# Issuing the FFN weight loads from ScalarE instead of SyncE, with a new order for all engines

## The chip, the cores and the metric

The kernel runs on one core of a Trainium2 chip. The metric is device time in microseconds (us) of one execution, lower being better. Shown of the kernel before are three timed runs, with a median of 195.04 us (192.67 to 195.28), and one profiled execution of its own, of 195.64 us, whose instructions span 193.9 us.

TensorE (PE) multiplies matrices, VectorE (DVE), ScalarE (ACT) and GpSimd (POOL) do element-wise work, and SyncE (SP) issues DMA transfers. ScalarE can issue them too. Each engine takes its own instructions strictly in the order in which they were written. Data that passes between engines is guarded by semaphores: an instruction carries the waits that must be met before it starts.

## What is computed

```
state = 0                                          # per batch (4) and head (8): 48 x 48
for t in range(768):
    cur   = (u * k[t]) outer v[t]
    y[t]  = r[t] @ (state + cur)
    state = w[t][:, None] * state + k[t] outer v[t]
x   = y as 3072 tokens x 384                       # 4 batches x 768 steps, 8 heads x 48
out = relu(x @ w_in) ** 2 @ w_out                  # w_in 384 x 2048, w_out 2048 x 384
```

So a recurrent attention layer is followed by a feed-forward network (FFN). Everything is given and returned in float32.

## The kernel before

**Tiling.** The 3072 tokens are cut into 24 steps of 128 tokens. For each step the attention part works on chunks: it loads w, r, k and v (192 KB each, L150), takes logarithms (`lw`) and cumulative sums by a matmul (`cum`), exponentials (`ci`, `exp`), scales r and k (`rd`), transposes them (`tr`, copied out by `rkt`), multiplies and masks (`p`, `pm0`, `pm1`), updates the state (`su`, `ac`, `ts`, `sn`) and forms y (`ys`, `ye`, plus the term with u by `ku`, `qp`, `q`, `vq`; summed in `ysb`). y is transposed (`yt`) and copied into `xT` (`xt`).

The FFN works on 17 blocks: ten of one step and seven of two. For a block, `m1:i:g` is a group of matmuls against `w_in` that fills one bank of PSUM (L405; 12 matmuls for a block of one step), `rl` takes it out with a relu (L414 on ACT, L416 on DVE), `gt` squares it, and `m2:i:mt:q` multiplies four of sixteen slices by `w_out` (L435). `os` scales the result out of PSUM and `store` writes it. There are two PSUM buffers for `m1`, so a third group can only start when the `rl` of the first has been done.

**FFN weights.** They come in eight loads of 768 KB. `ld:0:i` to `ld:3:i` (below wi0 to wi3; `load_wi`, L174 to L178) each bring a quarter of the columns of `w_in`; `ld:0:o` to `ld:3:o` (wo0 to wo3; `load_wo`, L180 to L184) each bring a quarter of the rows of `w_out`. They land in a staging pool of six float32 buffers, and `cast:i:g:j` (three per load) and `cast:o:g:j` (four per load) turn them into bf16 on ACT, DVE or POOL. Group g of `m1` in a block of one step needs the three casts of wi*g*, and quarter q of `m2` needs the four casts of wo*q*. As the pool has six buffers, wo2 and wo3 wait until wi0 and wi1 have been cast.

**Order.** A string, `ORDER`, lists every piece of work as a word; the function `tile_rwkv6_finch__then__act_relu_squared_kernel` reads it word by word under `tc.manual_schedule`. So each engine gets its instructions in the order of the words that concern it. A last letter picks the engine (A for ACT, V or W for DVE, G for POOL). `warm:n` puts n matmuls on zeros on PE as filler (`warm:n:1` has half a matmul more). All loads are issued from SP, in the order of the `ld` words; the `store` words stand in the same queue.

**Completion semaphores.** The framework gives every DMA one of eight completion semaphores in turn. An issue carries a wait on the previous DMA that had the same semaphore: that one must have landed. In the kernel before, all these DMAs are issued by SP (but for one half of the last store), so each waits for the eighth DMA ahead of it on its own queue. The raw tiles of w, r, k and v have seven buffers each.

Of the kernel before, what the change touches and what calls it, by code (L numbers as in the profile page):

```python
# [26 lines left out]
m1:2:2 gt:0:2:A cast:i:3:1:V ld:2:o rl:1:2:A cum:4 ye:3 ci:4 ac:3 m1:1:3 ld:3:o rl:2:2:A ku:4:G ysb:3 gt:1:2:A
ts:3 m1:2:3 ld:4:v rl:1:3:A gt:2:2:V qp:4:G yt:3 ld:5:w rl:2:3:A xt:3:V m1:0:3 exp:4 m1:3:0 sn:3:G q:4
rl:0:3:A rd:4 cast:o:0:1:G cast:o:0:2:A m1:3:3 cast:o:0:3:A cast:o:0:0:V gt:0:3:V tr:4 gt:1:3:A m2:0:0:0
gt:2:3:A rkt:4:V cast:o:1:1:G rl:3:0:A m2:1:0:0 ld:6:w cast:o:1:0:V rl:3:3:A cast:o:1:3:G ys:4 cast:o:1:2:V  # L30
p:4 gt:3:0:A m1:3:2 pm0:4 gt:3:3:A cast:o:2:1:G m1:3:1 cast:o:2:0:A pm1:4 rl:3:2:A cast:o:2:3:G m2:0:0:1
rl:3:1:V cast:o:2:2:G m2:1:0:1 ld:5:r gt:3:2:W gt:3:1:A ld:5:k m2:0:0:2 cast:o:3:2:G cast:o:3:0:A ld:7:w
cast:o:3:3:A m2:1:0:2 v:4:V vq:4:G ld:6:r cast:o:3:1:A ye:4 su:4 lw:5 m2:0:0:3 ysb:4 ac:4 ts:4 cum:5 m2:1:0:3
os:0:0:A ci:5 lw:6 ld:6:k yt:4 sn:4:V m2:2:0:0 exp:5 m2:2:0:1 xt:4:A ld:8:w os:1:0:A m2:2:0:2 rd:5 ku:5:G
ld:5:v m2:2:0:3 qp:5:G lw:7 cum:6 tr:5 os:2:0:V ld:6:v m2:3:0:0 ci:6 rkt:5:A q:5 m1:4:0 ld:9:w exp:6 ku:6:V
ys:5 m1:4:2 ld:7:r rl:4:0:A qp:6:G rd:6 m2:3:0:1 lw:8 store:0:0 gt:4:0:A m2:3:0:2 rl:4:2:V ld:7:k v:5:A vq:5:G
p:5 q:6 gt:4:2:A tr:6 ld:8:r pm0:5 m1:4:1 vq:6:G pm1:5 ld:8:k m2:4:0:0 rkt:6:V rl:4:1:A cum:7 v:6:V gt:4:1:A
ye:5 ld:7:v m2:3:0:3 ci:7 ysb:5 exp:7 m2:4:0:1 yt:5 os:3:0:A ld:9:r m1:4:3 xt:5:V rd:7 ku:7:G su:6 rl:4:3:A
m1:5:0 ld:9:k ac:6 qp:7:G p:6 gt:4:3:A sn:6 m1:5:2 ld:10:r rl:5:0:A pm0:6 ku:8:G lw:9 tr:7 pm1:6 ld:10:k
rl:5:2:A m2:4:0:2 gt:5:0:W rkt:7:A qp:8:G cum:8 ye:6 q:7 ld:11:r m2:4:0:3 ysb:6 gt:5:2:A vq:7:G m1:5:1 q:8  # L40
v:7:A ld:12:r ci:8 ys:7 yt:6 rl:5:1:A ku:9:G m2:5:0:0 xt:6:V store:1:0 exp:8 gt:5:1:W su:7 ld:11:k qp:9:G
m1:6:0 ac:7 rd:8 store:2:0 m2:5:0:1 rl:6:0:A ku:10:V m2:5:0:2 gt:6:0:A ld:8:v ts:7 qp:10:G p:7 q:9 m1:6:1
ld:9:v pm0:7 sn:7:G ld:12:k m1:5:3 pm1:7 rl:6:1:A tr:8 os:4:0:A q:10 ld:10:w gt:6:1:A m1:6:2 rl:5:3:A ku:11:G
cum:9 ye:7 ci:9 rl:6:2:A m2:6:0:0 ysb:7 store:3:0 gt:5:3:A qp:11:G m1:6:3 ld:13:r gt:6:2:W exp:9 m2:5:0:3
vq:8:G ld:11:w rl:6:3:V v:8:A m2:6:0:1 rd:9 rkt:8:A vq:9:G store:4:0 m2:6:0:2 q:11 v:9:G gt:6:3:A ys:8 yt:7
ld:13:k os:5:0:A p:8 ku:12:G xt:7:V m2:6:0:3 ld:10:v pm0:8 lw:10 su:8 pm1:8 qp:12:G m1:7:0 ld:14:r ac:8
os:6:0:V cum:10 ts:8 ye:8 rl:7:0:A m1:7:2 ld:14:k ci:10 sn:8:G gt:7:0:A tr:9 ysb:8 rl:7:2:A m1:7:1 q:12 exp:10
rkt:9:V ld:11:v m1:7:3 rl:7:1:A ku:13:G rd:10 yt:8 ys:9 rl:7:3:A ld:12:v m2:7:0:0 gt:7:2:A xt:8:V qp:13:G p:9
gt:7:3:A su:9 ld:12:w pm0:9 m1:8:0 vq:10:G ac:9 pm1:9 lw:11 m1:8:3 ld:13:w gt:7:1:A v:10:G ts:9 cum:11
rl:8:0:A q:13 ye:9 sn:9:G tr:10 ld:14:w rl:8:3:A ci:11 m1:8:1 ysb:9 gt:8:0:A ku:14:G store:5:0 m2:7:0:1  # L50
rkt:10:V exp:11 ld:15:r v:11:G m1:8:2 gt:8:3:A rd:11 ld:15:k qp:14:G yt:9 rl:8:1:A ys:10 m2:8:0:0 xt:9:V
v:12:A ld:13:v gt:8:1:W vq:11:G lw:12 su:10 p:10 ac:10 rl:8:2:V m2:7:0:2 vq:12:G lw:13 ld:16:r ts:10 gt:8:2:A
m2:7:0:3 pm0:10 sn:10:G lw:14 tr:11 pm1:10 os:7:0:A ld:17:r m2:8:0:1 rkt:11:A q:14 ye:10 cum:12 ld:16:k
m2:8:0:2 ysb:10 ku:15:G ci:12 yt:10 m2:8:0:3 ld:14:v xt:10:V exp:12 qp:15:G m1:9:0 os:8:0:A ld:18:r rd:12
m1:9:2 rl:9:0:A vq:13:G ys:11 q:15 ld:17:k m1:9:1 rl:9:2:A v:13:G gt:9:0:V gt:9:2:A su:12 p:11 ld:15:w
rl:9:1:A m1:9:6 pm0:11 ku:16:G ac:12 gt:9:1:A pm1:11 m1:9:3 ld:15:v rl:9:6:A sn:12 qp:16:G ye:11 m2:9:0:0
rl:9:3:A ysb:11 ld:18:k gt:9:6:A tr:12 gt:9:3:V vq:14:G q:16 m1:9:5 v:14:A store:6:0 rkt:12:A store:7:0
m2:9:1:0 ku:17:G rl:9:5:V ld:16:w m1:9:7 gt:9:5:A qp:17:G p:12 lw:15 ld:16:v yt:11 pm0:12 m1:9:4 rl:9:7:A
pm1:12 m2:9:1:1 ld:19:r rl:9:4:A xt:11:V ld:19:k cum:13 q:17 gt:9:4:A ye:12 m2:9:0:1 ci:13 v:15:A ysb:12
m2:9:0:2 exp:13 gt:9:7:W store:8:0 vq:15:G yt:12 ld:17:w m2:9:1:2 rd:13 xt:12:A ld:17:v m2:9:1:3 ku:18:V  # L60
cum:14 su:13 os:9:1:V qp:18:G ld:18:v m1:10:0 lw:16 ci:14 ac:13 m1:10:2 exp:14 ts:13 ld:20:r m2:9:0:3 q:18
# [447 lines left out]
```

## Time and profile before

| What | Value |
|---|---|
| Three timed runs | 192.67, 195.04, 195.28 us |
| Profiled execution, its own time | 195.64 us |
| Its span, first to last instruction | 193.9 us |
| PE busy | 186.4 us (96%) |
| DVE busy | 155.6 us (80%) |
| ACT busy | 141.5 us (73%) |
| POOL busy | 86.8 us (45%) |
| Moved by DMA | 30.24 MB |
| Mean granted TensorE clock | 1.000 |

The busy time of an engine is the time in which it executes; waiting and issuing DMAs are not in it. The span is divided into 40 slices in the page of the profile, and digits show in tenths how busy an engine was in each. A timeline shows an engine's instructions in order, runs of equal ones merged: start, length, line, tiles and count. SPq stands for the issue of a DMA by SP. In the chain of work that ended last, each step is followed back to what released it.

### The profile page before, as it was taken

What the parts mean: (1) busy time and instruction counts of PE and PEld (TensorE: products, weight loads), DVE (VectorE), ACT (ScalarE), POOL (GpSimd) and SP (SyncE); (2) the same over time, 40 slices, a digit from 0 to 9 for tenths busy, and PEclk for the clock granted to TensorE, in tenths of its full rate; (3) what the DMA queues carried; (4) which work ended last, traced back from release to release, by engine and by line L of the source; (5) the groups of instructions that cost most, each with busy time, mean ns of one, the idle gap of its engine ahead of it and who ended that gap; (6) DMA issues with size and microseconds to landing.
All of it is one profiled execution on the core that took longest, in us unless ns stands there. A gap on an engine that the chain in (4) does not pass through costs nothing.

```text
span 193.9 us, 5430 instructions
## 1 busy us (share of the span) xinstructions
PE 186.4 (96%) x2164; PEld 138.5 (71%) x2164; DVE 155.6 (80%) x285; ACT 141.5 (73%) x279; POOL 86.8 (45%) x115
## 2 busy tenths in 40 slices
...
DMA  6999998989998979899999899922000101001121
GB/s 135 211 236 317 260 248 247 367 192 198 212 220 172 243 154 224 169 206 224 228 242 205 173 206 205 229 51 81 3 0 21 63 0 59 29 3 41 41 73 52
DMA packets 107180, 30.24 MB, mean 156 GB/s; under 512 B 100370, under 2 KB 105619, under 8 KB 107155
## 3 DMA queue, kind: packets, MB, share of 16 engines
...
q10 hardware_dynamic: 144, 0.10, 0.2%
...
## 4 chain that ended last, share of the span: by engine, by line
PE 62%; SPq 16%; DMA 8%; POOL 5%; ACT 3%; issue 3%; DVE 1%; POOLq 0%
PE m L435 26%; PE m L405 22%; SPq L150 11%; DMA v_raw<-in_v_dram 5%; PE tr L302 4%; DMA rk_raw<-in_k_dram 3%; PE cp L314 3%; SPq L176 2%; SPq L182 2%; PE y L374 2%; PE tr L387 2%; POOL qprod L190 2%; POOL ku L190 2%; PE cp L272 1%; PE y L363 1%
## 5 line engine op out<-in xcount | busy, mean ns | idle before, releaser
L405 PE MATMUL m<-xT,wi_sb 128*128 128x128 bf16 (+1 forms) x816 | 75.3, 241 | 0.4 <-DVE xT L187 0.2
L435 PE MATMUL m<-wo_sb,gt 128*128 128x384 bf16 x384 | 73.1, 326 | 0.5 <-POOL wo_sb L187 0.5
L405 PEld LDWEIGHTS <-wi_sb 128*128 128x128 bf16 x816 | 59.2, 98 | 7.7 <-issue 0.5
L414 ACT ACTIVATE rl<-m 128x512 f16<-128x512 f32 x73 | 42.6, 594 | 10.6 <-PE m L405 9.8
L435 PEld LDWEIGHTS <-gt 128*128 128x128 bf16 x384 | 35.3, 98 | 18.3 <-issue 0.7
L426 ACT ACTIVATE gt<-rl 128x512 bf16<-128x512 f16 x61 | 37.5, 629 | 4.4 <-DVE rl L416 3.5
L326 DVE TENSOR_TENSOR pmT<-cp,tri_strict 128x512 bf16<-128x512 f32 x48 | 30.9, 683 | 3.9 <-PE cp L314 3.7
L190 POOL TENSOR_TENSOR ku<-rk_raw,u_bc 128x384 f32<-128x384 f32 x20 | 20.6, 1029 | 15.9 <-DMA rk_raw<-in_k_dram 14.9
L190 POOL TENSOR_TENSOR qprod<-rk_raw,ku 128x384 f32<-128x384 f32 x23 | 23.1, 1003 | 8.4 <-DVE ku L190 7.1
L283 ACT ACTIVATE cp<-cp 128x768 f32<-128x768 f32 x24 | 19.2, 799 | 10.2 <-DVE cp L276 10.1
L190 POOL TENSOR_TENSOR vq<-v_raw,q 128x384 f32<-128x384 f32 x22 | 18.4, 841 | 16.7 <-DVE y_sb L379 12.7
L293 DVE TENSOR_TENSOR rdec_buf<-rk_raw,cp 128x768 bf16<-128x768 f32 x24 | 22.8, 949 | 2.5 <-ACT cp L283 1.7
L190 POOL TENSOR_TENSOR S<-t_state,ac_buf 128x384 bf16<-128x384 f32 x13 | 11.1, 855 | 22.1 <-DVE t_state L349 22.0
L416 DVE TENSOR_SCALAR rl<-m 128x512 f16<-128x512 f32 x23 | 15.7, 686 | 6.0 <-PE m L405 4.9
L276 DVE SCALAR_TENSOR_TENSOR cp<-cp,lw_buf 128x384 f32<-128x384 f32 x24 | 13.4, 560 | 4.6 <-PE cp L272 4.6
L246 ACT ACTIVATE lw_buf<-w_raw 128x384 bf16<-128x384 f32 x24 | 12.4, 521 | 4.4 <-DMA w_raw<-in_w_dram 2.2
L453 PE MATMUL m<-warm 128*128 128x512 bf16 (+1 forms) x50 | 14.2, 424 | 1.3 <-DVE warm L220 1.3
L302 PE MATMUL tr<-ident,rdec_buf 128*128 128x128 bf16 x192 | 14.7, 219 | 0.1
L262 DVE TENSOR_REDUCE q<-qprod 128x8 f32<-128x384 f32 x24 | 13.1, 545 | 2.0 <-POOL vq L190 2.0
L379 DVE TENSOR_TENSOR y_sb<-vq,y 128x384 bf16<-128x384 f32 x24 | 13.2, 548 | 1.6 <-PE y L374 0.8
L302 PEld LDWEIGHTS <-rdec_buf 128*128 128x128 bf16 x192 | 11.9, 98 | 2.5 <-issue 0.7
L187 ACT COPY rkT<-tr 128x1024 bf16<-128x1024 bf16 x12 | 12.1, 1006 | 1.4 <-PE tr L302 1.4
...
## 6 DMA issues: line engine op xcount, KB each, us to landing
...
```

Source lines behind the costliest of these rows:

```text
L150: nc.sync.dma_start(out=dst, in_=src[b, :, c * C:(c + 1) * C, :].rearrange("h c d -> c h d"))
L190: {"V": nc.vector, "G": nc.gpsimd}[eng].tensor_mul(dst, a, b)
L283: nc.scalar.activation(cs[:, :, 0:DM], cs[:, :, 0:DM], AF.Exp)
L293: nc.vector.tensor_mul(rdec[:, :, :, 0:D], raw["rk", s][:], tiles.pop(("cs", s))[:, :, 0:DM].rearrange("p a (h d) -> p a h d", h=H))
L302: nc.tensor.transpose(ps_tr[:, i, p, :], rdec[:, i, 2 * p:2 * p + 2, :], ident[:])
L326: nc.vector.tensor_mul(tiles["pmT", s][:, e], tiles["p", s][:, e].rearrange("p (a t) -> p a t", a=HP), tri_strict[:, None, :].to_broadcast ...
L405: nc.tensor.matmul(ps1[:, j, :], wi_sb[:, kk, n * 128:(n + 1) * 128], xT[:, kk, s0 * C:s0 * C + width], start=(kk == 0), stop=(kk == KT - 1))
L414: nc.scalar.activation(rl[:], m1[:], AF.Relu, scale=RS)
L416: nc.vector.tensor_scalar(rl[:], m1[:], RS, 0.0, op0=ALU.mult, op1=ALU.max)
L426: nc.scalar.activation(gt, rl[:], AF.Square)
L435: nc.tensor.matmul(tiles["m2", i, mt][:], gt[:, n, mt * 128:(mt + 1) * 128], wo_sb[:, n, :], start=(n == 0), stop=(n == NT - 1))
L453: nc.tensor.matmul(ps[:, 0:256 if i == n else 512], warm[:, 0:C], warm[:, 0:256 if i == n else 512], start=True, stop=True)
```

## The change

Two things change. `load_wi` and `load_wo` issue their transfers by `nc.scalar.dma_start` where they had `nc.sync.dma_start`. So the eight weight loads stand in ACT's instruction order, and travel on ACT's DMA queue. And the string `ORDER` is a new one: the pieces of work are the same, but the order on every engine, the engine of many casts, relus and copies, and the fillers differ (50.5 filler matmuls in 13 places, where there were 48.5 in nine). No other line changes.

```diff
-ld:0:w ld:0:r warm:7 ld:0:k ld:1:r ld:0:u lw:0 cum:0 warm:9:1 ld:0:v ci:0 ld:1:w exp:0 ld:2:w rd:0 ub warm:2
-uc:A ld:2:r ld:1:k v:0:G tr:0 ld:2:k ku:0:G warm:3 rkt:0:V lw:1 qp:0:G su:0 lw:2 cum:1 ld:1:v warm:11 ac:0
-ci:1 sn:0 ld:2:v ku:1:G exp:1 q:0 ld:0:i rd:1 vq:0:G qp:1:V cum:2 tr:1 ku:2:G ld:3:w ci:2 warm:5 q:1 ld:1:i
-exp:2 rkt:1:V v:1:G ld:3:r rd:2 qp:2:G ld:3:k su:1 warm:1:1 ac:1 v:2:A ts:1 p:0 vq:1:G q:2 su:2 pm0:0 sn:1:G
-warm:4:1 ac:2 pm1:0 vq:2:G ld:2:i ts:2 ye:0 cast:i:0:0:A p:1 cast:i:0:1:G ysb:0 tr:2 cast:i:0:2:A sn:2:V ys:1
-lw:3 warm:5 pm0:1 rkt:2:A pm1:1 ld:3:v yt:0 ye:1 ld:3:i cast:i:1:1:G cast:i:1:2:A p:2 xt:0:V ysb:1 m1:0:0
...
+ld:0:w ld:0:u warm:5:1 ld:0:r ld:0:k ld:1:w ld:1:r ub lw:0 ld:0:v cum:0 uc:A warm:11 ci:0 ld:1:k exp:0 ku:0:G
+ld:1:v ld:0:i rd:0 lw:1 ld:2:w qp:0:V tr:0 q:0 cum:1 warm:5:1 rkt:0:A ld:2:r ci:1 exp:1 v:0:V ld:3:r vq:0:V
+su:0 warm:5 ac:0 rd:1 ku:1:G ld:3:w sn:0 p:0 qp:1:G v:1:A pm0:0 tr:1 warm:2 pm1:0 rkt:1:A q:1 ye:0 warm:0:1
+ysb:0 vq:1:G p:1 cast:i:0:2:A ld:2:k su:1 pm0:1 ys:1 cast:i:0:0:G ac:1 warm:2:1 pm1:1 lw:2 ld:3:k ld:1:i
+cast:i:0:1:G ts:1 ye:1 cum:2 ysb:1 yt:0 ld:2:v ld:2:i sn:1:G warm:3:1 ci:2 ld:3:i xt:0:V exp:2 ld:3:v yt:1
+m1:0:0 xt:1:V lw:3 m1:1:0 ld:4:w ld:0:o warm:5 rl:0:0:A rd:2 ku:2:G ld:4:r rl:1:0:A gt:0:0:A qp:2:G cum:3 tr:2
+gt:1:0:A ci:3 warm:3 rkt:2:V exp:3 ku:3:G q:2 ys:2 warm:4 rd:3 qp:3:G cast:i:1:0:A ld:4:k p:2 cast:i:1:2:G
+cast:i:1:1:A q:3 tr:3 pm0:2 ld:1:o v:2:G m1:1:1 ld:2:o rkt:3:V ld:3:o vq:2:G m1:0:1 pm1:2 rl:1:1:A su:2
+gt:1:1:V rl:0:1:A p:3 ye:2 cast:i:2:2:V cast:i:2:0:A warm:1:1 cast:i:2:1:V ac:2 ysb:2 m1:1:2 gt:0:1:A ts:2
...
     def load_wi(g):
         w_st["i", g] = stage_pool.tile([C, KT, GW], FP32, name="w_st")
-        nc.sync.dma_start(
+        nc.scalar.dma_start(
             out=w_st["i", g][:],
             in_=moe_w_in[:, g * GW:(g + 1) * GW].rearrange("(a p) f -> p a f", p=128))
 
     def load_wo(g):
         w_st["o", g] = stage_pool.tile([C, 4, DM], FP32, name="w_st")
-        nc.sync.dma_start(
+        nc.scalar.dma_start(
             out=w_st["o", g][:],
             in_=moe_w_out[g * 512:(g + 1) * 512, :].rearrange("(a p) d -> p a d", p=128))
```

With this, the eight completion semaphores are shared by two issuing engines. In the built program the weight loads, issued by ACT, take their turns between loads issued by SP, and each carries the wait for the DMA that had its semaphore before. The table names it, and what stands on ACT between one weight load and the next (w2 is the load of w for step 2, and so on):

| Weight load | Waits until this has landed | ACT's work up to the next one |
|---|---|---|
| wi0 | r0 | `lw:1`, `rkt:0`, `exp:1`, `ac:0`, `v:1`, `rkt:1`, `cast:i:0:2`, `ac:1`, `lw:2` |
| wi1 | r2 | none |
| wi2 | k2 | none |
| wi3 | v3 | `exp:2`, `lw:3` |
| wo0 | k4 | `rl:0:0`, `rl:1:0`, `gt:0:0`, `gt:1:0`, `exp:3`, `cast:i:1:0`, `cast:i:1:1` |
| wo1 | r5 | none |
| wo2 | r6, and POOL's cast of wi0 | none |
| wo3 | r7, and the casts of wi1 by ACT and POOL | `rl:1:1`, `rl:0:1`, `cast:i:2:0`, `ac:2`, and so on |

SP's loads now stand in this order: w0, u, r0, k0, w1, r1, v0, k1, v1, w2, r2, r3, w3, k2, k3, v2, v3, w4, r4, k4, v4, w5, w6, r5, k5, r6, k6, v5, r7, k7, v6, w7, w8, v7, r8, and then the first store. Those among them that wait for a weight load are w4 (for wi0), r5 (wi1), r6 (wi2), r7 (wi3), w7 (wo0), and the first store (wo1).

More of the change, by code (lines that the diff above doesn't have):

```diff
@@ L27 @@
[L27 to L61, printed above, removed]
@@ new lines @@
+m1:0:2 pm0:3 rl:1:2:A sn:2:G yt:2 pm1:3 cast:i:3:1:A ld:4:v cast:i:3:0:G ys:3 xt:2:A warm:1:1 rl:0:2:V
+cast:i:3:2:A m1:2:0 ld:5:w vq:3:G v:3:V gt:0:2:A m1:2:1 lw:4 gt:1:2:V ye:3 rl:2:0:A cum:4 su:3 ysb:3 rl:2:1:A
+m1:0:3 ci:4 gt:2:0:A m1:2:2 rl:0:3:V gt:2:1:A cast:o:0:1:G ld:6:w cast:o:0:0:A rl:2:2:V m1:2:3 cast:o:0:3:G
+ac:3 gt:0:3:A ts:3 m1:1:3 ld:5:r cast:o:0:2:G rl:2:3:A gt:2:2:V yt:3 sn:3:G rl:1:3:A m2:0:0:0 xt:3:V gt:2:3:W
+exp:4 m2:1:0:0 ku:4:G gt:1:3:A m1:3:0 rd:4 qp:4:G m1:3:2 rl:3:0:V cast:o:1:3:A tr:4 cast:o:1:2:A cast:o:1:0:V
@@ new lines @@
+cast:o:1:1:G m1:3:1 q:4 rl:3:2:A rkt:4:V gt:3:0:A m1:3:3 rl:3:1:A gt:3:2:V cast:o:2:2:G m2:0:0:1 cast:o:2:0:V
+cast:o:2:3:A cast:o:2:1:A ys:4 p:4 rl:3:3:A m2:1:0:1 pm0:4 gt:3:1:A pm1:4 m2:1:0:2 cast:o:3:0:G cast:o:3:1:A
+ld:5:k cast:o:3:3:V cast:o:3:2:A m2:0:0:2 gt:3:3:W v:4:A m2:0:0:3 ld:6:r vq:4:V ye:4 su:4 os:0:0:V lw:5 ld:6:k
+m2:1:0:3 ac:4 ysb:4 cum:5 ts:4 m2:2:0:0 os:1:0:A ld:5:v ci:5 sn:4:G yt:4 m2:2:0:1 exp:5 xt:4:V ld:7:r m1:4:0
+rd:5 ku:5:G m1:4:1 lw:6 ld:7:k rl:4:0:A m2:2:0:2 qp:5:V rl:4:1:A ld:6:v cum:6 gt:4:0:V tr:5 gt:4:1:A ci:6
@@ new lines @@
+qp:11:G rl:7:0:A m1:7:1 ac:8 q:10 m1:7:3 gt:7:0:A v:9:G ts:8 ld:12:w rl:7:1:A p:8 vq:9:G q:11 tr:9 os:5:0:A
+pm0:8 rl:7:3:A m1:7:2 sn:8:G ld:13:k pm1:8 v:10:A m2:7:0:0 vq:10:G lw:10 rkt:9:V store:3:0 rl:7:2:A ye:8
+ld:14:r cum:10 gt:7:3:V su:9 gt:7:1:A ci:10 m2:6:0:3 store:4:0 ac:9 gt:7:2:W lw:11 m2:7:0:1 ysb:8 exp:10
+ku:12:G ld:14:k m2:7:0:2 ts:9 rd:10 ys:9 yt:8 sn:9:G m2:7:0:3 v:11:A ld:15:r xt:8:A cum:11 ld:12:v qp:12:G
+tr:10 ci:11 os:7:0:A m1:8:0 rkt:10:V vq:11:G exp:11 ld:13:w m1:8:2 q:12 rl:8:0:A rd:11 su:10 rl:8:2:A m1:8:1
@@ new lines @@
+ku:13:G gt:8:0:A ld:13:v os:6:0:V p:9 lw:12 m1:8:3 pm0:9 qp:13:G rl:8:1:A ld:14:w pm1:9 m2:8:0:0 ac:10
+gt:8:2:A ts:10 ye:9 ld:15:w p:10 gt:8:1:A q:13 sn:10:G tr:11 rl:8:3:A ysb:9 m2:8:0:1 ld:15:k rkt:11:A pm0:10
+ku:14:G ys:10 m2:8:0:2 pm1:10 gt:8:3:A ld:14:v qp:14:G ye:10 cum:12 yt:9 ysb:10 m2:8:0:3 xt:9:A vq:12:G
+ld:16:r ci:12 ys:11 q:14 yt:10 exp:12 v:12:G xt:10:V ld:16:k lw:13 m1:9:0 rd:12 v:13:A vq:13:G m1:9:5
+store:5:0 rl:9:0:V ld:17:r p:11 rl:9:5:A tr:12 gt:9:0:V ld:15:v lw:14 pm0:11 m1:9:2 gt:9:5:A pm1:11 ld:17:k
@@ new lines @@
+rl:10:4:A ld:18:v ys:14 qp:20:V gt:10:7:A tr:15 v:16:G ld:22:r p:14 gt:10:4:A m2:10:1:1 pm0:14 rkt:15:A
+vq:16:G ld:22:k pm1:14 m2:10:1:2 q:19 m2:10:0:2 ld:19:v yt:13 ye:14 cum:16 xt:13:A m2:10:0:3 ysb:14 v:17:A
+ci:16 yt:14 ys:15 ld:20:v os:10:0:V m2:10:1:3 xt:14:A exp:16 vq:17:V m1:11:0 store:9:1 q:20 os:10:1:A ku:21:G
+store:10:0 su:15 rd:16 rl:11:0:A m1:11:1 ld:21:v ac:15 m1:11:3 gt:11:0:A qp:21:G ts:15 lw:18 rl:11:1:V p:15
+ld:23:r tr:16 rl:11:3:A sn:15:G pm0:15 gt:11:1:A m1:11:2 pm1:15 ld:21:w rkt:16:A m1:11:6 rl:11:2:V ld:22:w
@@ new lines @@
+cum:17 ku:22:G gt:11:3:A ye:15 rl:11:6:V su:16 m2:11:0:0 gt:11:2:A ci:17 qp:22:G ac:16 ysb:15 m2:11:1:0
+ld:23:w lw:19 gt:11:6:W exp:17 m1:11:5 vq:18:G ts:16 ld:22:v lw:20 ys:16 m1:11:4 rd:17 sn:16:G rl:11:5:A
+m2:11:1:1 store:10:1 v:18:A q:21 ld:23:v gt:11:5:A p:16 m1:11:7 rl:11:4:A pm0:16 ld:23:k gt:11:4:A pm1:16
+tr:17 m2:11:0:1 rl:11:7:V rkt:17:A cum:18 ye:16 ci:18 m2:11:1:2 gt:11:7:A v:19:G ysb:16 exp:18 yt:15 m2:11:0:2
+vq:19:G xt:15:A m2:11:0:3 rd:18 yt:16 ys:17 os:11:0:A q:22 m2:11:1:3 xt:16:A store:11:0 cum:19 m1:12:0
@@ new lines @@
+os:11:1:A ci:19 store:11:1 m1:12:4 exp:19 rl:12:0:V tr:18 rl:12:4:A gt:12:0:V m1:12:1 rd:19 rkt:18:A m1:12:3
+ku:23:G rl:12:1:V gt:12:4:A p:17 su:18 rl:12:3:A pm0:17 qp:23:G m1:12:2 ac:18 pm1:17 gt:12:1:A m1:12:7 sn:18
+lw:21 cum:20 gt:12:3:A rl:12:2:V ye:17 tr:19 v:20:G rl:12:7:A ci:20 m2:12:0:0 gt:12:2:A ysb:17 m1:12:6
+rkt:19:V exp:20 vq:20:G m2:12:1:0 gt:12:7:V rl:12:6:A yt:17 q:23 m1:12:5 gt:12:6:A rd:20 xt:17:A m2:12:1:1
+rl:12:5:A m2:12:0:1 gt:12:5:A p:18 su:19 pm0:18 m2:12:1:2 lw:22 pm1:18 ac:19 m2:12:0:2 ts:19 ye:18 p:19
```

77 lines of the change are left out of this document (37 added, 40 removed).

## The prediction

> **What bounds the kernel now.** I read the page first: the share of each engine, and the slices.
>
> ```profile
> span 193.9 us, 5430 instructions
> ...
> PE 186.4 (96%) x2164; PEld 138.5 (71%) x2164; DVE 155.6 (80%) x285; ACT 141.5 (73%) x279; POOL 86.8 (45%) x115
> ...
> DMA  6999998989998979899999899922000101001121
> ```
>
> PE is the bound of the whole, but the DMA engines are full from the second slice to the 26th (about 5 to 125 us). So in the first quarter two things can hold PE up: data that has not landed, and engines that have not prepared it. The windows by stage, with the DMA share and GB/s in the last two columns, and the timeline of PE say where that is over:
>
> ```profile
> 20.00:30.00 10.00, 9.68 (x164) 8.30 (x163) 9.92 (x18) 8.90 (x16) 5.63 (x8) 1.00 0.93 249
> 30.00:40.00 10.00, 9.88 (x148) 8.34 (x146) 8.94 (x18) 8.66 (x19) 4.75 (x6) 1.00 0.97 321
> 40.00:50.00 10.00, 9.23 (x90) 6.14 (x88) 6.20 (x12) 8.12 (x17) 4.86 (x7) 1.00 0.87 175
> 50.00:60.00 10.00, 10.00 (x145) 7.82 (x143) 8.80 (x16) 8.40 (x18) 6.55 (x7) 1.00 1.03 211
> 80.00:90.00 10.00, 9.46 (x116) 7.00 (x113) 8.08 (x16) 8.37 (x17) 8.95 (x12) 1.00 1.03 211
> 31.20:41.90 10.70, 10.13 (x137) 7.93 (x133) 8.80 (x16) 8.98 (x19) 6.17 (x9) 1.00 0.92 295
> ```
>
> ```profile
> 1.32 3.17 PE L453 MATMUL m<-warm 128*128 128x512 bf16 x7 [1.32 <-DVE warm L220]
> ...
> 10.80 2.54 PE L453 MATMUL m<-warm 128*128 128x512 bf16 x11
> ...
> 21.77 0.84 PE L405 MATMUL m<-xT,wi_sb 128*128 128x128 bf16 x12
> ...
> 44.26 0.81 PE L435 MATMUL m<-wo_sb,gt 128*128 128x384 bf16 x4
> ```
>
> The first useful `m1` stands at 21.77; before it PE runs mostly filler (`warm`). The row at 44.26 is `m2:1:0:3`, the end of the first two output tiles. By the words ahead of it, PE has then done the same in both kernels to within one `cum`: 16 `m1`, 7 `m2`, 5 `tr`, 5 `p`, 5 `su`, 5 `ye`, 4 `yt`. I use it as a **milestone**: it ends at 44.26 + 0.65 (four such matmuls back to back, in the chain below) = 44.9, and 193.9 - 44.9 = 149.0 us follow. So the question is when the changed kernel gets there. What follows is the same work with PE nearly always busy (10.00 of 10 at 50 to 60).
>
> **The change, part by part.** First the rate of transfers. A raw load of 192 KB (0.197 MB) at the 211 GB/s of 50 to 60, where almost nothing else is loaded, takes 0.93 us of the DMA engines. Between 31.2 and 41.9 nearly all that lands is wo0 to wo3: 0.786 MB at 295 GB/s is 2.67 us each. SP and the chain show how this adds up:
>
> ```profile
> 0.74 0.42 SPq L150 DMA_DIRECT2D w_raw<-in_w_dram  x1
> ...
> 10.78 0.86 SPq L176 DMA_DIRECT2D w_st<-in_moe_w_in_dram  x1
> ...
> 17.11 2.45 SPq L176 DMA_DIRECT2D w_st<-in_moe_w_in_dram  x1
> ...
> 27.80 4.24 SPq L182 DMA_DIRECT2D w_st<-in_moe_w_out_dram  x4
> ```
>
> ```profile
> 32.09 10.45 DMA v_raw<-in_v_dram
> ...
> 48.45 0.65 PE m L435 x4
> 49.10 0.67 PE m L405 x12
> ```
>
> ```profile
> 3.45 0.52 ACT L246 ACTIVATE lw_buf<-w_raw 128x384 bf16<-128x384 f32 x1 [1.44 <-DMA w_raw<-in_w_dram]
> ...
> 23.65 0.60 ACT L414 ACTIVATE rl<-m 128x512 f16<-128x512 f32 x1
> ```
>
> The first load lands at about 3.4 (ACT starts on it at 3.45), which is 2.45 + 0.93. v4 is the 20th raw load behind eight weights: 2.45 + 20 x 0.93 + 8 x 2.67 = 42.4, and the chain has it landing at 32.09 + 10.45 = 42.5. So a plain queue of 0.93 and 2.67 explains the first 42 us.
>
> *What is removed.* SP no longer issues eight weights; its rows at L176 and L182 are 0.4 to 2.5 us each. They are long because the queue is full, so this buys no transfer: zero, hidden by DMA engines that are at 0.93 to 1.03 anyway. Fillers ahead of the first `m1` are 35.5 instead of 48.5 matmuls: 13 x 231 ns (2.54 / 11) = 3.0 us that it may come earlier. That is worth something only if what follows keeps up.
>
> *What is added: waits on ACT.* An issue costs ACT little (SP's of the same transfer: 0.86 at 10.78, when the queue has room). But each of ACT's eight issues now carries a semaphore wait on a raw load, and ACT takes nothing behind it until it is met. SP shows what that is like, standing before stores:
>
> ```profile
> SPq L448 <- DVE o_sb L444: 25.8, 4, 11.5
> ```
>
> Up to 11.5 us in one piece. On SP that hid; on ACT, the relus, squares, exponentials and casts stand behind. Four waits tell. In the queue of SP, v3 is the 16th raw load, k4 the 19th, r5 the 23rd, r6 the 25th, r7 the 28th. With the weights that go before or beside them:
> - wi3 waits for v3: 2.45 + 16 x 0.93 + 3 x 2.67 (wi0 to wi2) = 25.3. Until then `exp:2` stands behind it, and nothing but the issue of wi2 lies between wi1 and wi3.
> - wo0 waits for k4: 2.45 + 19 x 0.93 + 4 x 2.67 = 30.8. `rl:0:0`, the first relu, comes after it; in the kernel before the second relu is at 23.65.
> - wo1 waits for r5: 2.45 + 23 x 0.93 + 5 x 2.67 = 37.2. ACT gets there by about 35.5, having done seven small pieces.
> - wo2 and wo3 wait for r6 and r7. For r7: 2.45 + 28 x 0.93 = 28.5 of start and raw loads, and wi0 to wo1, six weights, 16.0: **44.5**. Then 0.7 to issue: ACT is free again at 45.2.
>
> `rl:1:1` is the next on ACT. Both PSUM buffers of `m1` are full by then, `gt:1:1` and two casts of wi2 on DVE stand behind it, and `cast:i:2:0` is on ACT behind two relus. So PE cannot start `m1:1:2` before about 47, and has had nothing but four `m1` groups and three or four steps of attention until then.
>
> *How the weights share with raw loads* is not shown by the trace, where all go through one queue. From both sides: if raw loads always go first, r7 still needs wi3 (its own wait), so four weights are ahead: 2.45 + 26.0 + 10.7 = 39.2. If weights always go first, wo2 is too: seven, 47.2. I take six, the count of those whose waits were met well ahead of r7. [...]
>
> *From there to the milestone.* What ACT has to do from `rl:1:1` to the last cast of wo3 is 10 `rl`, 8 `gt`, 3 casts of wi, 7 of wo, one `exp`, one `lw`, two `ac` and one `xt`. The groups of ACT between 20 and 45 price them:
>
> ```profile
> L426 ACT ACTIVATE gt<-rl 128x512 bf16<-128x512 f16 x12 | 7.2, 629 | 0.1
> L414 ACT ACTIVATE rl<-m 128x512 f16<-128x512 f32 x12 | 7.0, 592 | 0.8 <-PE m L405 0.8
> L187 ACT CAST wo_sb<-w_st 128x384 bf16<-128x384 f32 x6 | 2.8, 511 | 1.7 <-DMA w_st<-in_moe_w_out_dram 1.7
> L187 ACT CAST wi_sb<-w_st 128x512 bf16<-128x512 f32 x3 | 1.8, 620 | 0.0
> L283 ACT ACTIVATE cp<-cp 128x768 f32<-128x768 f32 x2 | 1.6, 800 | 0.1
> L246 ACT ACTIVATE lw_buf<-w_raw 128x384 bf16<-128x384 f32 x3 | 1.6, 521 | 0.2 <-DMA w_raw<-in_w_dram 0.2
> ```
>
> 10 x 0.592 + 8 x 0.629 + 3 x 0.620 + 7 x 0.511 + 0.80 + 0.52, and 0.4 each as an estimate for `ac` and `xt`, the shortest, = 18.9. Two `m2` come behind (1.3): 20.2 us. PE alone has 12 `m1` at 0.67, 8 `m2` at 0.65 and some 2.5 of attention, 15.8 from 47 on: 18 after ACT's release. The kernel before took 44.9 - 23.65 = 21.3 from its second relu. I take 20, with 18 and 23 as ends.
>
> **The sum**, on the profiled execution: 45.2 + 20 = 65.2 for the milestone instead of 44.9, so 20.3 later; 195.64 + 20.3 = 215.9. On the other side DMAs go on while PE stands, so later stages have their data in time; PE stands for only about half a microsecond in 80 to 90 (9.46 of 10, the only window after 50 with such a gap), so that gives up to 0.5 back. An idle array also starts slowly: the first seven fillers took 453 ns each, later ones 231. If that happens after the stop at 47, 7 x 0.22 = 1.6 us, mostly hidden since ACT sets the pace there. Together about **215**, or 10% over. The profiled execution lies 0.6 over the median of 195.04, so against the median it's the same to within the noise; a change of 2% (3.9 us) is about what can be told from none.
>
> **The rivals.**
> - *Both queues flow side by side.* If weights cost the raw loads nothing, r7 lands at 28.5, ACT is free at 29.2, the milestone comes at 49.2, and the time is 195.64 + 4.3 = 199.9. For it: in the windows at 31 to 42 the share is 0.92, not 1. Against it: 0.93 to 1.03 with one queue alone leaves no room for a third more. [...] A partial gain would fall between 200 and 209. Chance 0.10.
> - *The waits are met before ACT gets there* (the other side: not slower). One mechanism: ACT itself arrives late at each weight load, by its own work, so that SP has the raw loads in and the queue on ACT runs as the order means it. It decides at wo3: ACT must be past it by 44.9 - 20 - 0.7 = 24.2. Then the first `m1` is earlier by up to the 3.0 us of filler, and the holes of PE from 20 to 50 (0.32, 0.12 and 0.77 by the windows) may close: 195.64 - 4.2 = 191.4. Against it: r7 cannot land before 28.5 even with no weight ahead. It would need raw loads faster than the 0.93 us that they take throughout. Chance 0.05.
> - *The change does nothing*, since the same DMA engines move the same bytes: the milestone stays at 44.9 and the time at 195.6. For it, the v4 sum above, which doesn't ask who issues. Against it, the relus now stand behind loads (k4, r7) that the kernel before had no need of so early: of its first 20 raw loads none is beyond step 4. Chance 0.05.
>
> **How the numbers follow.** My forecast, a release of ACT at 40 to 48 and a time of 209 to 222: 0.80. The rivals in their order: 0.10, 0.05 and 0.05. The ends of the main case: r7 at 39.2, with 18 after it, gives 39.9 + 18 = 57.9, 208.6; r7 at 47.2 with 23 gives 70.9, 221.6. The range should reach into the first rival, so 202 to 222. Slower by over 2%: 0.80 and the 0.10, all of which lies above 198.9: 0.90; within 2%: 0.05; faster: 0.05.
>
> **What the profile after would show.** On ACT, L176 and L182 with idle time before them, the longest before wo1 to wo3, put down to `rk_raw`'s DMA; `rl:0:0` at about 31 and `rl:1:1` at about 46; PE with a hole of some 8 us or more ahead of `m1:1:2`; the milestone at 58 to 71, then 149 us to the end. Shares of SP's issue in the chain should shrink. Wrong would be: ACT past wo3 by 30, landings closer than 0.93 us apart, a later stage that wins back over 2 us by its data being there, or one that loses as much since DVE or POOL can't keep the new order's pace.

## The result, and the profile after

The changed kernel takes 217.09 us (median of four runs, 215.80 to 219.37), the kernel before on the same chip 194.80 (four runs, 192.67 to 195.28). A run over 1.5% above the fastest of its kernel counts as slow, as that of 219.37 us does, and the ratios here and below are of fast runs alone, so that they need not equal the quotient of the medians: here 1.117, with an interval of 1.111 to 1.123. The profiled execution took 217.61 us. Its page has the span, the share of the engines, and the slices of PE's granted clock and of the DMA engines:

```profile
span 215.7 us, 5426 instructions
...
PE 191.3 (89%) x2168; PEld 142.1 (66%) x2168; DVE 158.2 (73%) x283; ACT 141.7 (66%) x283; POOL 84.3 (39%) x113
...
PEclk9999859656999999999999999999999999999999
DMA  6999999996004999997934299887100200100012
```

The span is 21.8 us longer, with the same work in it. In the fifth to the tenth slice (22 to 54 us), all but one, the clock falls, and behind them the DMA engines have two slices with next to nothing to do. The windows from 20 to 70 us (busy time of PE, PEld, DVE, ACT and POOL, then granted clock, DMA share and GB/s) show the same:

```profile
20.00:30.00 10.00, 4.69 (x41) 2.91 (x39) 2.80 (x5) 3.17 (x6) 4.12 (x6) 0.76 1.06 302
30.00:40.00 10.00, 5.71 (x75) 3.65 (x73) 3.53 (x6) 1.92 (x4) 0.83 (x1) 0.84 1.06 268
40.00:50.00 10.00, 2.53 (x24) 2.51 (x25) 3.23 (x7) 3.45 (x8) 1.45 (x3) 0.50 1.08 291
50.00:60.00 10.00, 9.89 (x142) 8.81 (x140) 7.42 (x14) 8.87 (x20) 5.51 (x8) 0.87 0.21 45
60.00:70.00 10.00, 10.00 (x122) 7.49 (x120) 8.59 (x19) 8.04 (x18) 2.97 (x5) 1.00 0.22 62
```

Between 20 and 50 us no engine is busy for more than six tenths of a window, while the DMA engines are full: everything waits, and what it waits for is transfers. PE does 12.9 us of work in these 30 us, where it did 28.8 before. The timeline of ACT says who is held first (start, length, instruction, tiles; in brackets the idle time before it and the releaser that the profile names):

```profile
17.98 7.82 ACTq L176 DMA_DIRECT2D w_st<-in_moe_w_in_dram  x2
25.84 0.80 ACT L283 ACTIVATE cp<-cp 128x768 f32<-128x768 f32 x1 [7.97 <-DMA v_raw<-in_v_dram]
...
27.63 0.38 ACTq L182 DMA_DIRECT2D w_st<-in_moe_w_out_dram  x1
28.05 1.09 ACT L414 ACTIVATE rl<-m 128x512 f16<-128x512 f32 x2 [0.99 <-DMA rk_raw<-in_k_dram]
...
35.77 10.00 ACTq L182 DMA_DIRECT2D w_st<-in_moe_w_out_dram  x3
45.82 1.09 ACT L414 ACTIVATE rl<-m 128x512 f16<-128x512 f32 x2 [13.90 <-DMA w_st<-in_moe_w_out_dram]
```

The issues of wi2 and wi3 stretch over 7.82 us and release `exp:2` when v3 lands. Those of wo1, wo2 and wo3 take 10.00 us from the first to the last. `rl:1:1` at 45.82 has been behind them since ACT's last piece of work at 31.9; the profile puts its 13.90 us down to the load `w_st` itself, whose issue stands right in front of it. What these issues waited for is in the chain of work that ended last (start, length, what; SP's r7 is issued at 37.66):

```profile
35.70 1.85 SPq L150
37.66 7.64 DMA rk_raw<-in_r_dram
...
45.40 0.37 ACTq L182
...
45.82 1.09 ACT rl L414 x2
46.90 0.52 ACT wi_sb L187
...
47.47 2.77 PE m L405 x24
```

r7, issued by SP, lands at 37.66 + 7.64 = 45.30. That lets ACT issue wo3 at 45.40, and half a microsecond after the landing it starts the relu that frees a PSUM buffer. Behind the relus comes the cast of wi2 (`cast:i:2:0`), the last thing that `m1:1:2` waits for. The other issues fit the table of waits as well: wo0 starts at 27.63 and k4 lands at 27.61, wo1 at 35.77 and r5 at 35.75, wo2 at 38.51 and r6 at 38.43. So each of the four follows the raw load that it waits for by 0.1 us or less, and a queue of ACT's that is merely full would not explain that. On PE the consequence is one long hole (timeline of PE):

```profile
19.79 1.50 PE L405 MATMUL m<-xT,wi_sb 128*128 128x128 bf16 x24
...
32.99 1.50 PE L405 MATMUL m<-xT,wi_sb 128*128 128x128 bf16 x24
...
47.47 2.77 PE L405 MATMUL m<-xT,wi_sb 128*128 128x128 bf16 x24 [11.76 <-ACT wi_sb L187]
...
51.31 2.10 PE L405 MATMUL m<-xT,wi_sb 128*128 128x128 bf16 x24
...
65.83 0.81 PE L435 MATMUL m<-wo_sb,gt 128*128 128x384 bf16 x4
```

The useful work begins 2.0 us earlier than before (19.79 for 21.77), and the milestone `m2:1:0:3` comes at 65.83 instead of 44.26. It ends at 65.83 + 0.65 = 66.48, and 215.7 - 66.48 = 149.2 us follow, against 149.0 before. So the whole loss lies ahead of the milestone.

### The profile page after: what moved, and what is told of

The parts are those of the page before. It is cut to its first block, busy times and chain, and to the rows that moved or that the text cites. A ratio compares the mean times of both kernels' runs of the same rounds, so it can differ in the third digit from the quotient of the medians.

```text
span 215.7 us, 5426 instructions
## 1 busy us (share of the span) xinstructions
PE 191.3 (89%) x2168; PEld 142.1 (66%) x2168; DVE 158.2 (73%) x283; ACT 141.7 (66%) x283; POOL 84.3 (39%) x113
## 3 DMA queue, kind: packets, MB, share of 16 engines
q1 hardware_dynamic: 103298, 23.50, 50.5%
## 4 chain that ended last, share of the span: by engine, by line
PE 68%; SPq 17%; DMA 5%; ACT 4%; DVE 3%; issue 1%; ACTq 0%; DVEq 0%
PE m L435 27%; PE m L405 26%; SPq L150 17%; PE tr L302 4%; DMA rk_raw<-in_r_dram 4%; PE cp L314 2%; ACT rl L414 2%; PE tr L387 2%; PE y L374 2%; DMA rk_raw<-in_k_dram 1%; PE y L363 1%; PE cp L272 1%; PE tr L340 1%; DVE cp L276 1%; DVE pmT L326 1%
## 5 line engine op out<-in xcount | busy, mean ns | idle before, releaser
L405 PE MATMUL m<-xT,wi_sb 128*128 128x128 bf16 (+1 forms) x816 | 76.2, 245 | 12.4 <-ACT wi_sb L187 11.8
L405 PEld LDWEIGHTS <-wi_sb 128*128 128x128 bf16 x816 | 61.3, 100 | 20.3 <-ACT wi_sb L187 12.1
L414 ACT ACTIVATE rl<-m 128x512 f16<-128x512 f32 x67 | 39.4, 598 | 26.4 <-DMA w_st<-in_moe_w_out_dram 13.9
L190 POOL TENSOR_TENSOR S<-t_state,ac_buf 128x384 bf16<-128x384 f32 x16 | 13.6, 848 | 50.3 <-DVE t_state L349 50.1
L283 ACT ACTIVATE cp<-cp 128x768 f32<-128x768 f32 x24 | 19.3, 805 | 10.5 <-DMA v_raw<-in_v_dram 8.0
L190 POOL TENSOR_TENSOR qprod<-rk_raw,ku 128x384 f32<-128x384 f32 x21 | 21.2, 1010 | 10.1 <-DVE ku L190 5.7
L190 POOL TENSOR_TENSOR vq<-v_raw,q 128x384 f32<-128x384 f32 x21 | 17.4, 829 | 18.8 <-DVE q L262 12.6
L428 DVE TENSOR_TENSOR gt<-rl 128x512 bf16<-128x512 f16 x25 | 12.0, 482 | 16.0 <-ACT rl L414 15.5
L416 DVE TENSOR_SCALAR rl<-m 128x512 f16<-128x512 f32 x29 | 19.9, 687 | 4.9 <-PE m L405 4.5
L453 PE MATMUL m<-warm 128*128 128x512 bf16 (+1 forms) x54 | 17.3, 457 | 1.3 <-DVE warm L220 1.3
L187 ACT COPY rkT<-tr 128x1024 bf16<-128x1024 bf16 x13 | 13.1, 1008 | 5.5 <-PE tr L302 5.5
L442 ACT ACTIVATE o_sb<-m 128x384 f32<-128x384 f32 x16 | 7.8, 489 | 9.9 <-PE m L435 9.7
```

What stands on the lines that cost most here:

```text
L190: {"V": nc.vector, "G": nc.gpsimd}[eng].tensor_mul(dst, a, b)
L283: nc.scalar.activation(cs[:, :, 0:DM], cs[:, :, 0:DM], AF.Exp)
L405: nc.tensor.matmul(ps1[:, j, :], wi_sb[:, kk, n * 128:(n + 1) * 128], xT[:, kk, s0 * C:s0 * C + width], start=(kk == 0), stop=(kk == KT - 1))
L414: nc.scalar.activation(rl[:], m1[:], AF.Relu, scale=RS)
L416: nc.vector.tensor_scalar(rl[:], m1[:], RS, 0.0, op0=ALU.mult, op1=ALU.max)
L453: nc.tensor.matmul(ps[:, 0:256 if i == n else 512], warm[:, 0:C], warm[:, 0:256 if i == n else 512], start=True, stop=True)
```

## The experiments

My theory was that the time goes into ACT's waits on completion semaphores, each of which holds all the work of ACT behind it until a raw load has landed. The rivals were that the new order is slow by itself, that a second queue slows the transfers, and that the cold array makes a part of it. Each time below is a median, each ratio is to the kernel before on the same chip. Milestones are the starts of the row of `m2:1:0:3` (44.26 before, 65.83 after); where an expectation gives one for the new order, it can be that of the `m2` behind it, 0.81 later, which decides nothing.

**The order alone.** The new order, with all loads issued from SP as before.

```diff
-        nc.scalar.dma_start(      # load_wi and load_wo
+        nc.sync.dma_start(
```

> The new order, with all eight weight loads issued by SP again. If the waits on ACT are the cause: no DMA stands on ACT, the weights run in SP's one queue as the words have it, 19 raw loads and 8 weights ahead of wo3's landing (2.45 + 17.7 + 21.4 = 41.5 us), first ACT relu before 30, milestone (end of m2:1:0:3) at 44 to 48, time 193 to 199. If the new order is itself the cause (which engine does what, fillers): the milestone stays past 55 and the time above 205.

Measured: 196.68 us, ratio 1.008 (1.004 to 1.013). For this kernel follow the window from 40 to 50, the row of `rl:1:1` in ACT's timeline, and the milestone in PE's:

```profile
40.00:50.00 10.00, 10.00 (x119) 7.36 (x117) 8.27 (x18) 8.01 (x18) 2.35 (x4) 1.00 0.93 186
```

```profile
26.93 1.33 ACT L414 ACTIVATE rl<-m 128x512 f16<-128x512 f32 x2 [1.75 <-PE m L405]
```

```profile
45.15 0.81 PE L435 MATMUL m<-wo_sb,gt 128*128 128x384 bf16 x4
```

The same word `rl:1:1` starts at 26.93 instead of 45.82, and waits 1.75 us for PE and for no transfer. So the order costs about 0.8%, and its 3.0 us of filler fewer ahead of the first `m1` buy nothing either: the milestone is 0.9 later than before, not earlier. The other 20 us come from where the weights are issued.

**The old order with the weights on ACT.** Only the two issuing lines are changed in the kernel before.

```diff
-        nc.sync.dma_start(        # load_wi and load_wo
+        nc.scalar.dma_start(
```

> The order of the kernel before, with the weight loads issued by ACT. In the built program wi3 then waits for k4, wo0 for wi3, wo1 for r6, wo2 for k6 and wo3 for w8. If the waits on ACT are the cause: ACT is past wo3 only at about 48 (2.45 + 29 raw loads x 0.93 + 7 weights x 2.67), against 34 where the kernel before has the same relu; milestone near 60, time 206 to 216. If the new order is the cause: 193 to 199. If two queues at once slow the raw loads, landings of raw loads come over 0.93 us apart wherever no weight is under way.

Measured: 204.9 us (two runs, 204.21 and 205.59), ratio 1.052 (1.039 to 1.065). It lies below what I expected. Rows of ACT's timeline, and the milestone in PE's:

```profile
29.40 1.14 ACT L187 CAST wi_sb<-w_st 128x512 bf16<-128x512 f32 x2 [4.06 <-DMA rk_raw<-in_k_dram]
...
43.26 0.40 ACTq L182 DMA_DIRECT2D w_st<-in_moe_w_out_dram  x1
43.76 0.60 ACT L414 ACTIVATE rl<-m 128x512 f16<-128x512 f32 x1 [2.50 <-POOL S L190]
```

```profile
55.39 0.81 PE L435 MATMUL m<-wo_sb,gt 128*128 128x384 bf16 x4
```

I had put ACT past wo3 at 48; it was past at 43.7, and here relus, squares and casts stand between the weight loads, so that the waits are taken in pieces (4.06 and 2.50 us in these rows) and not one behind the other. The profile names POOL for the 2.50, but w8, for which wo3 waits, was issued at 36.93 and landed at 43.19, right before wo3's issue at 43.26. My 48 had counted seven weights ahead of w8; only wi0 to wi3 had landed by then (wo0 at 43.42). Issuing from ACT hurts in either order, and more in the new one, which puts wo1 to wo3 together; that this is the reason isn't tried apart.

**Half of the change.** The new order with wi0 to wi3 on ACT and wo0 to wo3 on SP. The waits of the four on ACT then change too: wi1 waits for r2, wi2 for r3, wi3 for w3.

```diff
     def load_wo(g):
-        nc.scalar.dma_start(
+        nc.sync.dma_start(
```

> The new order; wi0 to wi3 issued by ACT, wo0 to wo3 by SP. In the built program the waits on ACT become r2, r3 and w3 (wi1 to wi3), all landed by about 18, and nothing of wo stands on ACT. If the waits on ACT are the cause: ACT is past its last weight load by 19, two queues are still in use, milestone at 43 to 48, time 192 to 199. If it is the use of two queues that costs: above 203. If the order: above 205.

Measured: 197.31 us, ratio 1.013 (1.006 to 1.020); the milestone is at 45.55. ACT's timeline:

```profile
18.09 1.97 ACTq L176 DMA_DIRECT2D w_st<-in_moe_w_in_dram  x2
20.11 0.80 ACT L283 ACTIVATE cp<-cp 128x768 f32<-128x768 f32 x1 [1.67 <-DVE cp L276]
...
21.23 1.26 ACT L414 ACTIVATE rl<-m 128x512 f16<-128x512 f32 x2
```

A second queue with half of the weights on it, and waits that are met when ACT gets to them: wi2 and wi3 take 1.97 us instead of 7.82. A queue on ACT isn't what costs; the raw loads that its issues wait for are.

**All weights issued by GpSimd, in the new order.** They then wait for semaphores of their own, and ACT issues nothing.

```diff
-        nc.scalar.dma_start(      # load_wi and load_wo
+        nc.gpsimd.dma_start(
```

> The new order, the eight weight loads issued by GpSimd at the same words. In the built program they have completion semaphores of their own, so no issue of a weight waits for a raw load, and no raw load for a weight; two queues are in use as in the changed kernel. If the semaphores that ACT's loads share with SP's are the cause: no hole in PE ahead of m1:1:2, milestone at 43 to 50 (POOL spends time on issuing), time 192 to 201. If two queues or the order are the cause: above 205.

Measured: 198.96 us, ratio 1.021 (1.013 to 1.028). Timeline of POOL, and the milestone:

```profile
16.88 0.81 POOL L176 DMA_DIRECT2D w_st<-in_moe_w_in_dram  x1
...
27.28 1.58 POOL L182 DMA_DIRECT2D w_st<-in_moe_w_out_dram  x2
```

```profile
46.19 0.81 PE L435 MATMUL m<-wo_sb,gt 128*128 128x384 bf16 x4
```

The second queue is there, the weights are all issued by 28.9, and the milestone is where the order alone has it, plus 1.0. The eight issues cost POOL about 0.8 us each. So a second queue speeds nothing ahead of the milestone. The 1.0 us can be POOL's issues; that isn't tried apart.

**The same with the old order,** and two halves of it in the old order: wi on ACT with wo on SP; and wi on SP with wo by GpSimd.

```diff
-        nc.sync.dma_start(        # load_wi and load_wo of the kernel before
+        nc.gpsimd.dma_start(
```

> The order of the kernel before, with the weight loads issued by GpSimd, so on a second queue and with semaphores of their own. If waits alone decide: the same as the kernel before or a little over it, by what POOL spends on eight issues of 0.85 us: 194 to 199. If two queues without the waits are a gain: the milestone below 44 and the time below 193.

```diff
     def load_wi(g):               # of the kernel before
-        nc.sync.dma_start(
+        nc.scalar.dma_start(
```

> The order of the kernel before, with wi0 to wi3 issued by ACT and wo0 to wo3 by SP. In the built program wi1 waits for k2 and wi2 for r3, both landed when ACT gets there, and wi3 for nothing that is late. If waits alone decide: as the kernel before within 2%, milestone at 43 to 46, 192 to 198. If a second queue for the first weights is a gain: below 192.

```diff
     def load_wo(g):               # of the kernel before
-        nc.sync.dma_start(
+        nc.gpsimd.dma_start(
```

> The order of the kernel before; wi0 to wi3 issued by SP as in it, wo0 to wo3 by GpSimd, on a second queue with semaphores of their own, so that no raw load waits behind them at its issue. If a second queue brings nothing where the DMA engines are full: 194 to 198, POOL's four issues costing 0 to 1.5. If taking the four weights out of SP's way closes PE's holes between 35 and 50 (1.3 us in all): 193 to 194.

Measured: all by GpSimd 196.98 us, ratio 1.010 (1.006 to 1.014), milestone 47.07, which is 2.8 later than before for a reason that isn't shown. With wi on ACT 198.38 us; its four runs spread from 196.67 to 200.78 and the profile is of the longest, so nothing is read from it. The ratio, 1.015 (1.009 to 1.020), doesn't tell it from no change by 2%, and the median is above the 192 to 198 that I had expected. With wo by GpSimd 194.84 us, ratio 0.998 (0.995 to 1.001), and the milestone is at 44.44, where it was. None of the three beats the kernel before: a second queue that holds nobody up is worth nothing here.

**The wo loads later.** In the changed kernel wo1 to wo3 go eight pieces of ACT's work later. Their waits become v5, r7 and k7.

```diff
-cast:i:1:1:A q:3 tr:3 pm0:2 ld:1:o v:2:G m1:1:1 ld:2:o rkt:3:V ld:3:o vq:2:G m1:0:1 pm1:2 rl:1:1:A su:2
+cast:i:1:1:A q:3 tr:3 pm0:2 v:2:G m1:1:1 rkt:3:V vq:2:G m1:0:1 pm1:2 rl:1:1:A su:2
...
-m1:0:2 pm0:3 ... ys:3 xt:2:A warm:1:1 rl:0:2:V
+m1:0:2 pm0:3 ... ys:3 xt:2:A warm:1:1 ld:1:o ld:2:o ld:3:o rl:0:2:V
```

> The changed kernel with the words of wo1, wo2 and wo3 moved eight pieces of ACT's work later (behind xt:2); all else in its order. In the built program they then wait for v5, r7 and k7. If the cost is what stands behind the wait in ACT's order: ACT does rl:1:1 to xt:2 before about 40, stands until about 46, and reaches the milestone 4 to 5 us earlier (eight pieces at 0.5 to 0.6 us), at 61 to 63; time 211 to 214. If the time is set by when the weights have landed, or by the total of transfers: not earlier than the changed kernel, 216 to 219, since wo1 to wo3 are issued no sooner.

Measured: 211.71 us, ratio 1.085 (1.081 to 1.090), so 5.4 us of the loss are gone. ACT's timeline, and the milestone:

```profile
34.94 1.33 ACT L414 ACTIVATE rl<-m 128x512 f16<-128x512 f32 x2 [2.44 <-PE m L405]
...
41.76 2.36 ACTq L182 DMA_DIRECT2D w_st<-in_moe_w_out_dram  x3
44.16 0.62 ACT L187 CAST wi_sb<-w_st 128x512 bf16<-128x512 f32 x1 [4.97 <-DMA rk_raw<-in_k_dram]
```

```profile
60.20 0.81 PE L435 MATMUL m<-wo_sb,gt 128*128 128x384 bf16 x4
```

`rl:1:1` comes at 34.94, 10.9 us earlier, and waits for PE. The wait isn't gone: it stands eight pieces later (4.97 us), and the wo loads themselves land later. Of the 10.9 us the milestone keeps 5.6. Of these 5.6, 1.7 come from ACT being free earlier (44.16 for 45.82): the last load that it waits for is now k7, which lands at 43.59, where r7 landed at 45.30. The other 3.9 are the eight pieces that ACT now does ahead of the wait. That is the behaviour of a wait that holds what is behind it, with the same queues, the same bytes and the same order but for three words.

**Is it the cold array?** PE's granted clock is 0.50 in the window from 40 to 50. In the changed kernel I put fillers into the two holes, to keep the array at work: 28 matmuls instead of 5 behind `m1:1:0`, and 50 instead of 1.5 ahead of `m1:1:2`.

```diff
-... ld:0:o warm:5 rl:0:0:A ...
+... ld:0:o warm:28 rl:0:0:A ...
...
-... cast:i:2:0:A warm:1:1 cast:i:2:1:V ac:2 ysb:2 m1:1:2 ...
+... cast:i:2:0:A warm:50 cast:i:2:1:V ac:2 ysb:2 m1:1:2 ...
```

> The changed kernel with more filler matmuls in the two stretches in which PE stands: 28 instead of 5 ahead of tr:2, and 50 instead of 1.5 ahead of m1:1:2 (at 216 ns each some 5 and 10.5 us). The waits of ACT are untouched. If the slow TensorE clock after the standstill costs on the path: the granted clock near 1.0 and the groups m1:1:2 and m1:0:2 in 1.5 instead of 2.8 us, milestone 1 to 2.5 us earlier, time 214.5 to 216. If ACT alone sets the pace there, so that the slow clock is hidden: the same time as the changed kernel, 216 to 218. If the standstill itself were the clock's doing: far below 210.

Measured: 218.5 us (215.62 to 219.43), ratio 1.111 (1.104 to 1.119). The profile is of the run of 215.62 us, with a mean clock of 1.000, and doesn't stand for the others. So the changed kernel and the same fillers ran once more, on one chip:

> The changed kernel once more, as the yardstick for the next one on the same chip: 215.5 to 219, granted clock 0.95 to 0.96.

> The changed kernel with the two standstills of PE filled, again, beside the changed kernel itself. If the slow TensorE clock after the standstill costs on the path: 1 to 2.5 us below the changed kernel of these same rounds, as the milestone of the first profile had it. If ACT's pace hides it, or the fillers cost as much as they bring: within 0.7 us of it.

Measured: 217.22 us for the changed kernel, ratio 1.115 (1.111 to 1.120), and 217.79 with fillers, 1.116 (1.111 to 1.122). No gain in time. The timelines of PE, first of the first filled run, then of the second, and ACT's of the second:

```profile
34.83 10.95 PE L453 MATMUL m<-warm 128*128 128x512 bf16 x50
47.54 1.59 PE L405 MATMUL m<-xT,wi_sb 128*128 128x128 bf16 x24 [1.75 <-ACT wi_sb L187]
...
63.95 0.81 PE L435 MATMUL m<-wo_sb,gt 128*128 128x384 bf16 x4
```

```profile
40.50 10.74 PE L453 MATMUL m<-warm 128*128 128x512 bf16 x49
51.08 1.50 PE L405 MATMUL m<-xT,wi_sb 128*128 128x128 bf16 x24
...
67.40 0.81 PE L435 MATMUL m<-wo_sb,gt 128*128 128x384 bf16 x4
```

```profile
31.60 0.39 ACTq L182 DMA_DIRECT2D w_st<-in_moe_w_out_dram  x1
...
47.04 1.09 ACT L414 ACTIVATE rl<-m 128x512 f16<-128x512 f32 x2 [11.14 <-DMA rk_raw<-in_r_dram]
```

From the start of `m1:1:2` to the end of the milestone it is 64.60 - 47.54 = 17.1 us in the one and 68.05 - 51.08 = 17.0 in the other, as with the order alone (28.8 to 45.8); in the changed kernel it is 66.48 - 47.47 = 19.0, and in its second profile 65.81 - 47.52 = 18.3. So the cold array costs 1.3 to 1.9 us in these executions, and in the first the two slow rows of the timeline carry it: (2.77 - 1.50) + (2.10 - 1.50) = 1.87. The second filled run gives it back and more. There k4 landed late, ACT came to wo0 at 31.60 instead of 27.63, and the fillers began 5.7 us later and were still running when ACT let go at 47.04: `m1:1:2` came at 51.08. Fillers of a fixed number can't fit a hole whose start moves by 4 us. That this is what happened in the timed runs too isn't shown, and it can't be all of it: three of these six filled runs had a granted clock of 0.998 to 1.000 from end to end, and took 216.38, 217.25 and 217.27 us, where the changed kernel took 217.22 at 0.953 to 0.960. So the price of the cold array is seen in profiles up to the milestone, and not in the times.

## Why the prediction was right, and where it was off

The direction and the mechanism held, and 217.09 us lies in the range, 2.1 over the 215.0. Step by step:

| Step | Predicted | Measured |
|---|---|---|
| wi3 past its wait for v3 | 25.3 | 25.8 (17.98 + 7.82) |
| wo0 past its wait for k4, `rl:0:0` | 30.8, about 31 | 27.6 and 28.05; 29.1 and 29.6 in the second profile of the changed kernel; 31.6 and 32.0 in the second filled run |
| wo1 past its wait for r5 | 37.2 | 35.8 |
| r7 lands | 44.5 (39.2 to 47.2) | 45.30 |
| ACT free, `rl:1:1` | 45.2, about 46 | 45.82 |
| `m1:1:2` | not before about 47 | 47.47 |
| hole of PE ahead of it | 8 or more | 11.76 |
| ACT's release to the end of the milestone | 20 (18 to 23) | 66.48 - 45.82 = 20.7 |
| from there to the end | 149.0 | 149.2 |
| given back later | up to 0.5 | nothing |

- **The cause** is shown, not argued: three ways to take the waits away from ACT or to have them met when it gets there (the weights on SP, half of them on SP, all by GpSimd) bring the milestone from 65.83 back to 45.2 to 46.2, with the new order in place. And moving three issues by eight pieces takes away 5.4 us, though part of that comes from waits that are met earlier. In the changed kernel itself, four issues start within 0.1 us of the landing that they wait for.
- **The queue sum** was right to 0.8 us at its last term by luck, through two errors that nearly cancel. The term "six weights ahead of r7" was one short: wo2 lands at 45.3, with r7, so seven are ahead. And 2.67 us per weight was too much: 28.5 of start and raw loads leave 45.30 - 28.5 = 16.8 for seven, 2.40 each, if raw loads keep their 0.93. With 2.40 the sum for r5 is 2.45 + 23 x 0.93 + 5 x 2.40 = 35.8, as measured. That weights get ahead of raw loads is seen early, too. The time from issue to landing, of k1 issued at 5.80 and of wi0 issued at 6.50 (tile views of the changed kernel), then of k1 in the kernel before:

```profile
L150 SPq DMA_DIRECT2D rk_raw<-in_k_dram x1: 1101/1101/1101, 5.8 to 5.8; - x1
...
DMA to landing us min/median/max: 7.0/7.0/7.0
```

```profile
L176 ACTq DMA_DIRECT2D w_st<-in_moe_w_in_dram x1: 436/436/436, 6.5 to 6.5; - x1
...
DMA to landing us min/median/max: 5.9/5.9/5.9
```

```profile
DMA to landing us min/median/max: 3.8/3.8/3.8
```

  wi0 lands at 12.4, ahead of k1 at 12.8, though it was issued later and is four times as large; k1 takes 7.0 us for the 3.8 of before. In the DMA view of 9 to 10.5 us, 228 packets of ACT's queue moved 0.47 MB and took 82.4% of the engines' time, beside 247 packets of SP's with 0.05 MB and 15.9%: about as many packets from each, and nine to ten times the bytes for the weights. That isn't so throughout: from 20 to 22 us it is 279 packets of ACT's and 488 of SP's, with 0.54 and 0.09 MB. I had worked out both counts, 44.5 with six weights ahead and 47.2 with seven, and put the lower one into the sum; it was seven, and only the price per weight kept 47.2 from being right.
- **k4 at 30.8** was 3.2 us too late in the profiled execution and 0.8 too early in another one. The sum counted wi3 among the weights ahead of k4; ACT issued wi3 only at 25.4, 2.2 us before k4 landed, and the six weight loads whose landing this trace tells took 5.7 to 7.3 us. Without it the sum is 2.45 + 19 x 0.93 + 3 x 2.67 = 28.1. Why k4 came later in two other profiles stays open. Its landing moved the hole's start and left its end: ACT was idle again from 31.9, since wo1 to wo3 wait for r5, r6 and r7.
- **"Mostly hidden"** was wrong of the cold array. I had priced it at up to 1.6 us and let ACT cover it. It is up to 1.9 us, and in the open: ACT's release to the milestone takes 45.80 - 26.93 = 18.9 us with the order alone, and 20.7 here (19.9 in the second profile). The bound from ACT's work, 20.2, was too high for a warm array, so that the sum came out nearly right with the wrong share in it, which again is luck.
- **"DMAs go on while PE stands"** was half of the story. They do until 50 us (291 GB/s), and then they nearly stop (45 and 62 GB/s). SP's waits and its timeline:

```profile
SPq L448 <- DVE o_sb L444: 29.0, 5, 18.4
```

```profile
46.45 1.22 SPq L150 DMA_DIRECT2D rk_raw<-in_r_dram  x1
66.15 0.37 SPq L448 DMA_DIRECT2D out_dram<-o_sb  x1
66.56 1.09 SPq L150 DMA_DIRECT2D rk_raw<-in_k_dram  x1
```

  SP has issued r8 by 47.7 and stands for 18.4 us before the first store, with all later loads behind it. I had quoted such a wait, 11.5 us of the kernel before, as harmless on SP, and hadn't asked how long it would become. It stayed harmless: 149.2 us follow the milestone. But nothing came back either, and the 0.5 us and the rounding that brought 215.9 down to 215 should have been left out.
- **A sign that failed:** SP's issue was to shrink in the chain that ended last. It has 17% of it (16% before): the chain runs through SP's raw loads up to r7, which ACT now waits for. The weights that left SP do show by line: L176 and L182 had 2% each of the chain before and are gone from SP, but the raw loads (L150) went from 11% to 17% and took their place.

Of the rivals, "side by side" needed r7 at 28.5, and "the change does nothing" needed ACT's relus early; both fall by the rows above. "The waits are met before ACT gets there" can be tried by the order alone and by half the change, where the waits are met: that gives 196.7 and 197.3 us, not 191.4. So even with its condition met it wouldn't have been faster; the new order isn't worth 4 us without the waits, nor any.
